# Attention and SwiGLU block on one core: twelve early head pairs laid four tokens to a partition and turned by TensorE, weight sums contiguous in DRAM, reciprocals between two transposes, and new durations in the planner

## The chip, the core and the metric

The kernel runs on one core of a Trainium2 chip. The metric is the device time of one launch in microseconds (us). The kernel before took a median of 1483.65 us in three runs (1482.71 to 1483.81). A separate, profiled execution took 1484.42 us; its span, from the first to the last instruction, was 1482.6 us, so 1.8 us lie around the span. Times called "at 85.2" are us from the start of that span.

## What is computed

Queries, keys and values have shape (8 batches, 12 heads, 448 tokens, 64). Each head is normalised and attended, the heads are joined to rows of 768, and the 3584 rows go through a SwiGLU block with 1536 hidden columns. All inputs but the weights are float32; the three weight matrices arrive as float64 words, which the kernel reads as pairs of 32-bit words and rounds itself.

```python
def rmsnorm(x, g):
    rms = np.sqrt(np.mean(x * x, axis=-1, keepdims=True) + 1e-06)
    return x / rms * g
q_n, k_n = (rmsnorm(q, g_q), rmsnorm(k, g_k))
scores = scale * np.matmul(q_n, k_n.transpose(0, 1, 3, 2))
attn = np.exp(scores - np.max(scores, axis=-1, keepdims=True))
attn = attn / (np.sum(attn, axis=-1, keepdims=True) + 1e-09)
x = np.matmul(attn, v)                      # then (B,H,S,D) -> (B*S, H*D)
g = x @ w_gate
return (g / (1.0 + np.exp(-g)) * (x @ w_val)) @ w_out
```

## The kernel before

**Stages.** Two heads of one batch are a *pair*; there are 48 pairs, m = 0 to 47. The first 12 pairs (EARLY, batches 0 and 1) are computed before any SwiGLU work. Then come four blocks, one for every two batches. A block has 120 up products (L1400: NG = 4 groups of hidden columns by 15 sums by gate and value, four matmul records each) and 30 down products (L1574: 15 sums by two halves of the output columns, eight records each). The products work on 15 sums and differences of input blocks with 15 sums and differences of weight blocks instead of the 18 plain ones, so the weights must be turned into "sides": `convert` loads 9 blocks of 128 columns, rounds them on ScalarE and VectorE, forms 11 sums on GpSimd and stores 15 blocks to DRAM (`up_sides`, `down_sides`). There are 24 conversions: 6 beside the early pairs, 18 beside the first block. `load_sides` (L1360) reads the sides back for each group of products, five sums at a time for up products and two for down products. The 36 late pairs run beside the down products of the blocks before the last.

**One pair** (`attention`). Queries and keys are loaded, squared (ScalarE, L767), summed (VectorE), turned into 1/rms (ScalarE L682 and L683, VectorE L688 to L690), scaled on GpSimd, and brought to the layout with the 64 head columns on the partitions, as KT and QT. Then four score tiles (j = 3, 0, 1, 2; L912), exponentials on ScalarE (L927), weighted values (L988) and column sums of the exponentials (L1019). For an early pair the sums are inverted on VectorE (L1054) and spread over the partitions by a TensorE product with a 0/1 matrix (L1062); for a late pair ScalarE spreads them by eight copies (L1072). ScalarE and VectorE add the two halves of the weighted values (L1077, L1080) and VectorE multiplies by the inverse (L1084).

There are two layouts on the way in. For a pair in NATURAL, which is pairs 0 and 1, a tile is [112 partitions, 2 heads, 4 tokens by 64]: one DMA with runs of 1 KB for queries and one for keys (L732). VectorE sums over 64 columns (L787). TensorE transposes four blocks of keys and four of queries into one PSUM tile of the ring `st` (L853); VectorE copies the keys out (L859), ScalarE the queries with the gain `gg` (L861). For all other pairs a tile is [4 strips of 32 columns, 14 by 32 tokens]: four DMAs with runs of 128 bytes each for queries and keys (L737); the sum over a head's 64 columns lies in two strips, so ScalarE swaps strips by four copies (L803) and VectorE adds (L807); the scaled tiles are turned by VectorE's 32 by 32 transposes (L865), and ScalarE scales the queries into QT (L868). The ring `st` has two tiles of two banks, and the score tiles take turns in it.

**At the start** TensorE is kept busy by four dummy products of 512 columns on the squared keys' input of pair 0 (L770). The keys of pair 0 are loaded from ScalarE's queue, everything else from SyncE's.

**Order.** No engine's order is written by hand. Every piece is given to a planner (`Order.add`: engine, duration, due time, what it comes after, which ring places it takes). `Order.run` plays the program with these durations and emits, again and again, the piece that can start first; among pieces that can start, the one with the earliest due time less `rank` (60 for early pairs, 20 for some conversions). Pieces of the same `group` on TensorE are kept together. Each engine executes in the emitted order, and a piece waits for what it needs. `SWITCH` is what a change of matmul mode costs in the play, `slack` a hop between engines; transfers were played as kilobytes over 300 GB/s plus 1.8 us.

Of the kernel before, what the change touches and what calls it, by code (L numbers as in the profile page):

```python
# [359 lines left out]

class Order:
# [10 lines left out]
    SWITCH = dict(PE=0.17, ACT=1.3)  # L372

    def __init__(self, pools, begin):
        self.begin = begin
        self.pools = {name: [None] * n for name, n in pools.items()}
        self.turn = dict.fromkeys(pools, 0)
        self.users = {}
        self.pieces = []
        self.free = {}  # L380
        self.port = 0.0
        self.dma = 0.0
        self.last = {}
        self.mode = {}

    def add(
        self, engine, us, when, emit, after=(), takes=(), uses=(), port=False, kb=0, group=None,
        mode=None, early=None, rank=0.0, slack=0.1,
    ):
        piece = dict(  # L390
            engine=engine, us=us, when=when, emit=emit, takes=takes, port=port, kb=kb,
            group=group, mode=mode, early=early, rank=rank, slack=slack,
# [10 lines left out]
    def start(self, piece):  # L403
# [6 lines left out]
        for before in piece["after"]:  # L410
            if before["end"] is None:
                return None
            at = max(at, before["end"] + piece["slack"] * (before["engine"] != piece["engine"]))
        for name, _ in piece["takes"]:
            old = self.pools[name][self.turn[name] % len(self.pools[name])]
            for user in self.users.get(old, ()):
                if user["end"] is None:
                    return None
                at = max(at, user["end"] + 0.1)
        return at  # L420

    def run(self, lookahead=400):
# [3 lines left out]
        while any(left.values()):  # L426
            best = None
            for engine, pieces in left.items():
# [15 lines left out]

                late = 0.7 if engine == "POOL" else 0.0
                if choice and (
                    best is None
                    or choice[0] + late < best[0] - 0.3
                    or choice[0] + late < best[0] + 0.3
                    and self.key(choice[1]) < self.key(best[1])  # L450
                ):
                    best = (choice[0] + late, choice[1])
# [8 lines left out]
            if piece["mode"] and self.mode.get(piece["engine"]) != piece["mode"]:  # L461
                end += self.SWITCH[piece["engine"]]
                self.mode[piece["engine"]] = piece["mode"]
                if piece["mode"] in self.begin:
                    self.begin[piece["mode"]]()
            self.last[piece["engine"]] = piece
# [3 lines left out]
            if piece["kb"]:  # L470
                self.dma = max(self.dma, end) + piece["kb"] / 300.0
                end = self.dma + 1.8
# [5 lines left out]
def fast(  # L478
# [60 lines left out]
    NATURAL = (0, 1)  # L539
# [9 lines left out]
        qk=4, v=2, t=2, QT=2, KT=2, e=4, ea=7, eh=2, sums=1, inv=1, rd=1, rows=3, st=2, at=2, ss=2,  # L549
# [65 lines left out]
    up_sides = [dram.tile([P, 15, 2, NC2, P], F32, name=f"up_sides{g}") for g in range(NG)]  # L615
    down_sides = dram.tile([P, 15, 2, NG, P], F32, name="down_sides")
# [58 lines left out]
    def inverse_root(m, sums, of, when, rank=0.0):  # L675
# [9 lines left out]
        def improve():  # L685
# [7 lines left out]
            "ACT", 0.5, when, estimate, after=[sums], uses=[("ss", m)], takes=[("rr", m)],  # L693
# [3 lines left out]
            "DVE", 0.45, when + 1.0, improve, after=[first], uses=[("ss", m), ("rr", m)],  # L697
# [9 lines left out]
    def attention(m):  # L707
# [19 lines left out]
        def load(x, src):  # L727
            def emit():
# [11 lines left out]
            both = m == 0 and src is k  # L740
            queue = nc.scalar if both else nc.sync
            return add(
                "ACT" if both else "SP", 0.5 if natural else 1.4 if both else 2.4, ready - 28.0, emit, takes=[("qk", (m, x))], kb=224, early=25.0,
# [15 lines left out]
        load_v = add("SP", 2.4, ready - 16.0, load_values, takes=[("v", m)], kb=256, early=25.0)  # L759

        def square(x):
# [6 lines left out]
            if m == 0 and x:  # L768
                for _ in range(4):
# [3 lines left out]
        for x in range(2):  # L773
            squares.append(
                add(
                    "ACT", 0.53, ready - 18.0, lambda x=x: square(x),
# [28 lines left out]
        def both():  # L805
# [6 lines left out]
            "DVE", 1.1, ready - 17.0, summed, after=squares, uses=[("t", m)], takes=[("ss", m)]  # L812
        )
        if not natural:
            sums = add("ACT", 0.9, ready - 16.0, swap, after=[sums], uses=[("ss", m)])
            sums = add("DVE", 0.15, ready - 15.0, both, after=[sums], uses=[("ss", m)])
# [6 lines left out]
        def scale(x):  # L823
            if natural:
# [16 lines left out]
                "POOL", 1.0, ready - 9.0, lambda x=x: scale(x), after=[rr], port=True,  # L841
# [32 lines left out]
        if natural:  # L874
            of_turned = ("st", (m, "turned"))
            kt, qt = [
                add(
                    "PE", 0.8, ready - 6.0, lambda x=x: turn(x), after=[scaled[1 - x]],
                    uses=[("t", m)] + [of_turned] * (1 - x), takes=[of_turned] * x, mode="full",
                )  # L880
                for x in (1, 0)
            ]
            kt = add(
                "DVE", 0.64, ready - 5.0, lambda: drain(1), after=[kt], takes=[("KT", m)],
# [3 lines left out]
                "ACT", 0.6, ready - 5.0, lambda: drain(0), after=[qt, gains], takes=[("QT", m)],  # L888
# [3 lines left out]
            "DVE", 0.62, ready - 6.0, lambda: transpose(1), after=scaled[:1], takes=[("KT", m)],  # L892
# [3 lines left out]
            "DVE", 0.62, ready - 6.0, lambda: transpose(0), after=scaled[1:],  # L896
# [3 lines left out]
            "ACT", 0.65, ready - 5.0, queries, after=[qt, gains], uses=[("qk", (m, 0))],  # L900
# [42 lines left out]
        for j in (3, 0, 1, 2):  # L943
# [4 lines left out]
                "PE", 0.41 if half else 0.76, when, lambda j=j: scores(j),  # L948
# [5 lines left out]
                "ACT", 0.5 if half else 0.92, when + 1.0, lambda j=j: exps(j),  # L954
# [3 lines left out]
            if j in (1, 2) and not early:  # L958

                def more_sums(j=j):  # L960
                    if j == 1:
# [5 lines left out]
                        "POOL", 2.15, when + 2.0, more_sums, after=[ex[j], ex[0], *adds[-1:]],  # L967
# [62 lines left out]
        for j in range(NJ):  # L1030
            half = j == NJ - 1
            last = add(
                "PE", 0.41 if half else 0.76, when + 0.01 * j, lambda j=j: weighted(j),
# [8 lines left out]
            "PE", 1.68 if early else 0.42, when + (0.05 if early else 0.3), total,  # L1042
# [10 lines left out]
        def invert():  # L1053
            nc.vector.reciprocal(take("rd", m, [P, Q]), tiles[den])  # L1054
# [27 lines left out]
        def divide():  # L1082
# [4 lines left out]
            "ACT", 0.55, when + 3.0, copy_sums, after=[last, up_done.get(b // 2 - 1)], uses=at[:1]  # L1087
# [683 lines left out]
```

## Time and profile before

| | before |
|---|---|
| median of three runs | 1483.65 us |
| profiled execution, its span | 1484.42 us, 1482.6 us |
| TensorE (PE) busy | 1435.1 us, 97% of the span |
| VectorE (DVE), ScalarE (ACT), GpSimd (POOL) busy | 914.8, 680.7, 416.0 us |
| mean TensorE clock granted | 0.992 |
| moved by DMA | 193.30 MB in 409457 packets, of them 316804 under 512 bytes |
| up products, two groups of 960 matmul records | 400.6 and 401.0 us busy |
| down products, three groups, 960 records | 177.2, 152.1 and 50.4 us busy |

The busy time of TensorE is the union of modelled intervals: a matmul record lasts longer than the distance to the next one, so a stretch can be called fully busy and yet not run at its best pace. For that the distance between starts is the better measure: in the trace four records of 64 by 64 matmuls of 448 columns start together every 0.375 us, and a 128 by 128 record of 448 columns starts every 0.376 us. "Idle before" in a group of instructions says how long the engine had nothing before them, and what ended that wait.

### The profile page before, as it was taken

Reading aid. Unit: us, or ns where it says so; the run is one execution under the profiler, and the core shown is the slowest. Engines: PE = TensorE matmul, PEld = TensorE weight load, DVE = VectorE, ACT = ScalarE, POOL = GpSimd, SP = SyncE. Lnnn points to the kernel's source line nnn. Section 1 sums busy time; section 2 is a strip of 40 time slices with the busy share of each in tenths; the row PEclk is TensorE's granted clock in tenths of the full one; section 3 lists DMA queues with packets and bytes.
Section 4 is the critical chain, followed back from the end, with each engine's and each line's share of the span. In section 5 each row is a group of like instructions: output and inputs, shape, how many; then the busy total and the mean of one; then the engine's idle time right before and its main releaser. Section 6 shows DMA issues by size and latency. Waiting matters only on the chain.

```text
span 1482.6 us, 19482 instructions
## 1 busy us (share of the span) xinstructions
PE 1435.1 (97%) x6696; PEld 680.7 (46%) x6696; DVE 914.8 (62%) x1403; ACT 680.7 (46%) x1358; POOL 416.0 (28%) x470
## 2 busy tenths in 40 slices
PE   6989999999999999999999999999999999999998
PEld 2434554443444455544444445554444445555553
DVE  3878897877978544355886733454786753432533
ACT  5864544437775321445767422354676532122100
POOL 3545585636444100012534200011343410000000
PEclk8999999999999999999999999999999999999999
DMA  6677999974453431533344432352444442222235
GB/s 166 160 162 215 294 331 335 289 213 92 98 117 84 111 107 71 144 98 89 78 110 107 101 118 72 110 132 77 97 101 103 89 123 85 80 98 73 83 98 107
DMA packets 409457, 193.30 MB, mean 130 GB/s; under 512 B 316804, under 2 KB 391428, under 8 KB 403204
## 3 DMA queue, kind: packets, MB, share of 16 engines
q1 hardware_dynamic: 397840, 190.35, 47.8%
q10 hardware_dynamic: 11380, 1.61, 0.7%
q8 instruction: 55, 0.90, 0.3%
q14 instruction: 54, 0.44, 0.1%
q0 software_dynamic: 128, 0.00, 0.0%
HBM read 157.29 MB, written 34.60 MB: 129 GB/s over the span
## 4 chain that ended last, share of the span: by engine, by line
PE 73%; ACT 3%; DVE 3%; issue 1%; DMA 1%; SPq 1%; ACTq 0%; DVEq 0%
PE mm L1574 22%; PE mm L1400 20%; PE at L1400 20%; PE st L912 6%; PE at L988 5%; PE st L1019 1%; ACT spare L1072 1%; ACT es L927 1%; SPq L737 1%; DVE rd L1054 1%; DVE ss L807 0%; DMA work<-in_k_dram 0%; DMA out_dram<-spare 0%; DVE ss L793 0%; ACT ss L803 0%
## 5 line engine op out<-in xcount | busy, mean ns | idle before, releaser
L1400 PE MATMUL at<-xs,ws 128*128 128x448 f32 x960 | 400.6, 540 | 4.3 <-DVE v L1346 3.1
L1400 PE MATMUL mm<-xs,ws 128*128 128x448 f32 x960 | 401.0, 540 | 3.6 <-DVE spare L1348 2.2
L1400 PEld LDWEIGHTS at<-xs,ws 128*128 128x128 f32 x960 | 181.9, 190 | 184.8 <-issue 172.1
L1400 PEld LDWEIGHTS mm<-xs,ws 128*128 128x128 f32 x960 | 181.6, 190 | 184.3 <-issue 172.0
L834 POOL TENSOR_TENSOR work<-work,rr 128x448 f32<-128x448 f32 x92 | 101.8, 1126 | 480.1 <-DVE rr L690 353.3
L1574 PE MATMUL mm<-gt,ws 128*128 128x448 f32 x448 | 177.2, 545 | 0.0
L912 PE MATMUL st<-work 64*64 64x448 f32 (+1 forms) x1536 | 156.4, 514 | 18.0 <-ACT es L927 7.5
L1344 DVE TENSOR_TENSOR gt<-gt,mm 128x448 f32<-128x448 f32 x64 | 39.7, 620 | 184.2 <-PE mm L1400 181.9
L1574 PE MATMUL mm<-hs,ws 128*128 128x448 f32 x384 | 152.1, 545 | 0.9 <-DVE ss L688 0.9
L927 ACT ACTIVATE es<-st 128x896 f32<-128x896 f32 x129 | 114.1, 912 | 54.3 <-PE at L988 42.6
L932 POOL TENSOR_TENSOR sums<-es 128x896 f32<-128x896 f32 x36 | 75.8, 2104 | 196.0 <-PE st L1019 83.4
L1474 ACT ACTIVATE st<-gt 128x448 f32<-128x448 f32 x96 | 52.3, 546 | 168.9 <-DVE gt L1348 90.3
L1072 ACT COPY spare<-rd 32x224 f32<-32x224 f32 x288 | 108.1, 375 | 35.4 <-DVE rd L1054 31.1
L1574 PEld LDWEIGHTS mm<-gt,ws 128*128 128x128 f32 x448 | 82.9, 190 | 84.2 <-issue 80.6
L988 PE MATMUL at<-es,v 64*64 64x448 f32 x1032 | 109.9, 544 | 2.7 <-DVE ss L688 2.5
L1342 ACT COPY gt<-mm 128x448 f32<-128x448 f32 x80 | 42.5, 532 | 140.4 <-PE mm L1400 140.4
L1574 PEld LDWEIGHTS mm<-hs,ws 128*128 128x128 f32 x384 | 71.1, 190 | 72.9 <-issue 70.6
L912 PEld LDWEIGHTS st<-work 64*64 64x64 f32 x1536 | 50.8, 135 | 98.8 <-issue 38.1
L1342 ACT COPY v<-at 128x448 f32<-128x448 f32 x96 | 51.1, 532 | 85.1 <-PE at L1400 81.0
L932 POOL TENSOR_TENSOR sums<-sums,es 128x896 f32<-128x896 f32 x36 | 78.7, 2186 | 2.8
L865 DVE STREAM_TRANSPOSE work<-work 128x448 f32<-128x448 f32 x92 | 56.6, 627 | 25.5 <-POOL work L834 22.8
L988 PEld LDWEIGHTS at<-es,v 64*64 64x64 f32 x1032 | 39.5, 134 | 63.0 <-issue 58.7
(161 smaller groups left out, 1589.1 us busy)
## 6 DMA issues: line engine op xcount, KB each, us to landing
ws<-up_sides SPq DMA_DIRECT2D x32, 1024.0 KB, 5.0
ws<-down_sides SPq DMA_DIRECT2D x16, 1024.0 KB, 5.0
ws<-down_sides SPq DMA_DIRECT2D x28, 512.0 KB, 4.3
ws<-up_sides SPq DMA_DIRECT2D x16, 768.0 KB, 4.4
work<-in_q_dram SPq DMA_DIRECT2D x184, 56.0 KB, 2.4
work<-in_k_dram SPq DMA_DIRECT2D x184, 56.0 KB, 2.4
out_dram<-spare SPq DMA_DIRECT2D x168, 56.0 KB, 1.9
v<-in_v_dram SPq DMA_DIRECT2D x96, 96.0 KB, 2.6
```

The costliest lines, as they stand in the source:

```text
L834: nc.gpsimd.tensor_tensor(out=tiles["t", m][:, x], in0=tiles["qk", (m, x)], in1=rr.to_broadcast([P, NC, C]), op=ALU.mult,)
L865: nc.vector.transpose(to, tiles["t", m][:, x].rearrange("p c f -> p (c f)"))
L912: nc.tensor.matmul(st[ds(D * x, D), h, 0:n], tiles["KT", m][rows, ds(P * j + D * of_keys, D)], tiles["QT", m][rows, ds(Q * of_queries, n)] ...
L927: nc.scalar.activation(e, tiles["st", (m, j)][:, :, 0 : S * width(j) // P], AF.Exp)
L932: nc.gpsimd.tensor_tensor(out=to, in0=tiles["e", (m, 0)] if j == 1 else to, in1=e, op=ALU.add)
L988: nc.tensor.matmul(tiles["at", (m, x)][ds(D * h, D), queries], tiles["v", m][rows, j, h], tiles["e", (m, j)][rows, h], start=j == 0, stop= ...
L1072: nc.scalar.copy(inv[ds(D * h + C * to, C), ts(x, Q)], tiles["rd", m][ds(D * h + C * x, C)])
L1342: nc.scalar.copy(to, ps)
L1344: nc.vector.tensor_tensor(out=to, in0=old, in1=ps, op=ALU.add)
L1400: nc.tensor.matmul(ps(), w[:, at, which, c], xs[:, SLOT[x], c], start=fresh and c == 0, stop=c == NC2 - 1, skip_group_check=True,)
L1474: nc.scalar.activation(take(*act, [P, 2, TB])[:, 0, 0:S], to, AF.Silu)
L1574: nc.tensor.matmul(banks[s][:, 0:S], w[:, at, s, g], where[x][:, g], start=fresh and g == 0, stop=g == NG - 1, skip_group_check=True,)
```

## The change

The diff does six things.

1. `NATURAL` holds all 12 early pairs instead of two. For the ten pairs 2 to 11, queries and keys come by one DMA each; the swap and its addition, the two VectorE transposes and the ScalarE scaling go; eight TensorE transposes, one VectorE copy and one ScalarE copy with the gain come.
2. The keys of pair 0 are loaded from SyncE's queue, and the dummies are three products on the queries of pair 0 instead of four on its keys.
3. The sides lie in DRAM with the 15 sums innermost but one ([P, 2, NC2, 15, P] instead of [P, 15, 2, NC2, P]). A conversion stores one run of 7680 bytes per partition, loaded sides come in four (up) or eight (down) runs of 512 bytes for each sum in a group. The tiles in SBUF and the matmuls' weight addresses follow.
4. For every pair, early or late, VectorE transposes the sums, inverts one column in 32 (7 per partition instead of 224), and transposes the broadcast back.
5. The planner's durations are new for almost every piece, a hop between engines costs 0.15, a mode switch 0.1, and a transfer is played by its issues, its packets and eight places in flight. GpSimd's handicap of 0.7 is gone, and the search for an engine's next piece ends at the first one that can start at once.
6. All conversions have rank 20; before, the first six had rank 0.

```diff
+def transfer(rows, size):
+    return rows * (6.64 + 0.045 * min(size, 4096)) / 16000.0
...
-    SWITCH = dict(PE=0.17, ACT=1.3)
+    SWITCH = dict(PE=0.1, ACT=1.3)
+    HOP, ISSUE, LANDING, PLACES = 0.15, 0.54, 2.0, 8
...
-            at = max(at, before["end"] + piece["slack"] * (before["engine"] != piece["engine"]))
+            at = max(at, before["end"] + self.HOP * (before["engine"] != piece["engine"]))
...
                     if choice is None or at < choice[0] - 0.4:
                         choice = (at, piece)
-
-                late = 0.7 if engine == "POOL" else 0.0
+                    if choice[0] <= self.free.get(engine, 0.0):
+                        break
...
+            for us in piece["moves"]:
+                place = self.issues % self.PLACES
+                at = max(at, self.landed[place]) + self.ISSUE
+                self.dma = max(self.dma, at - self.ISSUE + self.LANDING) + us
+                self.landed[place] = self.dma + 0.35
+                self.issues += 1
+                end = at
...
-    NATURAL = (0, 1)
+    NATURAL = (0, 1, 2, 3, 4, 5, 6, 7, 8, 9, 10, 11)
...
-    up_sides = [dram.tile([P, 15, 2, NC2, P], F32, name=f"up_sides{g}") for g in range(NG)]
-    down_sides = dram.tile([P, 15, 2, NG, P], F32, name="down_sides")
+    up_sides = [dram.tile([P, 2, NC2, 15, P], F32, name=f"up_sides{g}") for g in range(NG)]
+    down_sides = dram.tile([P, 2, NG, 15, P], F32, name="down_sides")
...
-            both = m == 0 and src is k
+            both = m == 0 and src is k and not natural
...
-            if m == 0 and x:
-                for _ in range(4):
+            if m == 0 and x == 0:
+                for _ in range(3):
                     nc.tensor.matmul(banks[0], chosen[0:R, 0], of, start=True, stop=True)
...
         def invert():
-            nc.vector.reciprocal(take("rd", m, [P, Q]), tiles[den])
+            rd, rc = take("rd", m, [P, Q]), take("rc", m, [P, Q // C])
+            nc.vector.transpose(rd, tiles[den])
+            nc.vector.reciprocal(rc, rd.rearrange("p (c i) -> p c i", i=C)[:, :, 0])
+            every = rc.rearrange("p (c one) -> p c one", one=1).to_broadcast([P, Q // C, C])
+            nc.vector.transpose(rd, every)
...
         inv = add(
-            "DVE", 1.52, when + 4.0, invert, after=[all_sums], uses=[] if of_bank else [den],
-            takes=[("rd", m)],
+            "DVE", 1.05, when + 4.0, invert, after=[all_sums], uses=[] if of_bank else [den],
+            takes=[("rd", m), ("rc", m)],
         )
         if early:
             inv = add(
-                "PE", 0.82, when + SPREAD, spread_by_product, after=[inv], mode="full", slack=1.0,
+                "PE", 0.75, when + SPREAD, spread_by_product, after=[inv], mode="full",
...
-        rank = 20.0 if by_bank else 0.0
+        rank = 20.0 if by_bank else 20.0
...
         last = add(
-            "SP", 0.6, when, lambda: nc.sync.dma_start(to, sides), after=[last], kb=960,
+            "SP", 0.6, when, lambda: nc.sync.dma_start(
+                to.rearrange("p x f -> p (x f)"), sides.rearrange("p x f -> p (x f)")
+            ), after=[last], moves=[transfer(2 * P, 3840)],
         )
...
-                src = sides[:, ds(first + here[0], size)]
-                nc.sync.dma_start(to[:, ds(i, size)], src.rearrange("p x a b f -> p x (a b f)"))
+                src = sides[:, :, :, ds(first + here[0], size)].rearrange("p a b x f -> p (a b) (x f)")
+                nc.sync.dma_start(to[:, :, ds(i, size)].rearrange("p n x f -> p n (x f)"), src)
```

## Prediction

> **What bounds the kernel now.** I read the page first, then busy time by stage, then what TensorE waited for in the first stage, then the timeline of the gaps.
>
> ```profile
> span 1482.6 us, 19482 instructions
> ...
> PE 1435.1 (97%) x6696; PEld 680.7 (46%) x6696; DVE 914.8 (62%) x1403; ACT 680.7 (46%) x1358; POOL 416.0 (28%) x470
> ```
>
> TensorE sets the end. A gain must come from its idle time, its slow clock or less work for it. This is the table by stage; columns are wall time, busy time of each engine, granted clock, DMA share, GB/s:
>
> ```profile
> 0.00:20.00 20.00, 11.06 (x39) 5.33 (x40) 6.59 (x20) 6.54 (x12) 7.46 (x18) 0.91 0.72 161
> 20.00:40.00 20.00, 14.42 (x144) 5.35 (x146) 9.50 (x19) 15.45 (x31) 3.68 (x4) 0.83 0.62 162
> ...
> 60.00:80.00 20.00, 17.42 (x201) 8.16 (x194) 16.50 (x28) 15.73 (x30) 13.21 (x22) 1.00 0.79 185
> 80.00:100.00 20.00, 16.84 (x174) 7.40 (x170) 12.33 (x20) 13.62 (x27) 9.39 (x16) 0.83 0.71 161
> ...
> 140.00:330.00 190.00, 184.28 (x490) 92.23 (x489) 156.59 (x234) 84.79 (x118) 118.93 (x228) 1.00 0.95 293
> 330.00:480.00 150.00, 145.16 (x967) 60.69 (x966) 122.03 (x178) 106.66 (x248) 77.11 (x46) 1.00 0.46 102
> 480.00:1440.00 960.00, 953.88 (x3931) 458.21 (x3930) 523.02 (x797) 397.62 (x821) 158.02 (x98) 1.00 0.37 99
> ```
>
> From 480 to 1440 only 6 us of 960 are idle. The gaps, and a clock of 0.83, lie in the first 140 us, where ten of the twelve early pairs are edited. What TensorE waited for there (total, times, longest):
>
> ```profile
> PE mm L770 <- DMA work<-in_k_dram: 6.8, 1, 6.8
> PE st L912 <- ACT es L927: 5.1, 2, 3.2
> PE st L912 <- ACT more L927: 4.1, 2, 3.2
> PE st L912 <- ACT work L861: 2.6, 2, 2.1
> PE at L988 <- DVE ss L688: 2.5, 1, 2.5
> ```
>
> The exponentials named are not the cause; they were only last. The timeline has it:
>
> ```profile
> 13.41 0.93 PE L853 MATMUL st<-ident,work 112*128 112x112 f32 x8
> ...
> 15.77 0.63 ACT L861 ACTIVATE work<-st,gg 128x448 f32<-128x448 f32 x1 [3.13 <-DVE gg L1680]
> 16.45 1.05 PEld L912 LDWEIGHTS st<-work 64*64 64x64 f32 x16 [2.32 <-ACT work L861]
> ```
>
> ```profile
> 87.86 0.58 ACT L767 ACTIVATE work<-work 128x448 f32<-128x448 f32 x1 [1.84 <-DMA work<-in_k_dram]
> 87.95 2.10 SPq L737 DMA_DIRECT2D work<-in_q_dram  x4
> 88.35 0.53 ACT L927 ACTIVATE more<-st 128x448 f32<-128x448 f32 x1
> ```
>
> At 87.86 ScalarE stands before a square whose keys have not landed; the exponentials behind it start late, and TensorE has been idle since 85.2. At 73.2 it is the same (square of late keys at 71.72, then 2.6 us idle). At the head, first scores are at 16.45 because the dummies hold TensorE to 13.41 and `gg` comes late on VectorE.
>
> Distances between matmul starts give the account from 16.45 to the first up product at 139.9, 123.5 us. Four 64 by 64 records of 448 columns start every 0.375 us, so a pair takes 2.63 (scores) + 2.63 (weighted) + 1.5 (sums) + 0.75 (spread) = 7.5 us: 90 for twelve, 0.8 for the transposes of pair 1. Gaps over 0.3 us and stretches at half clock are 22.6. The remaining 10 are mode switches and short waits, 0.8 a pair.
>
> **What the Trainium skill says.** TensorE: Matmul & The Clock Gate, "What's actually happening": after an idle window of about 3.4 us the clock falls to half. The trace agrees: after idling 3.4 us at 24.8 and 3.3 us at 85.2 the distance is 0.75 instead of 0.375 us, which cost some 2.7 and 3.0 us. "Part 4: PE-mode transpose" of that page adds that transposes do not count as activity; no trace of before can show that, as only 16 were made. DMA: Bandwidth & Descriptors, "Specifications", names 512 bytes as the least size for line rate. Here a 128-byte packet took 12.5 ns in the first 140 us and a 1024-byte one 52, so 1 KB goes in 52 instead of 100 ns. SBUF — State Buffer, "SBUF: two separate sides": a VectorE operation with two SBUF inputs and a GpSimd one exclude each other; the tiny L807 agrees, 400 ns mean where undisturbed ones took 190.
>
> **The change, part by part**, in us of the end; each estimate with both ends.
>
> *Head.* Keys of pair 0 were issued on ScalarE's queue at 1.61 behind the gains and landed after 5.1 us; now they are SyncE's second transfer, ahead of the values. Queries landed after about 3. Keys may land at 4.5 to 6.7; I take 5.5. From landing to scaled queries took 5.4 us for the first pair's last scale (6.71 to 12.1). The six dummy records at half clock, 0.857 each, end at about 9 instead of 13.4, before that. Then transposes 0.4, copy 0.63, hops: scores at 12.9, a gain of 3.5. With `gg` late again it is 0, with keys at 4.5 it is 5.5. **−3.5 (−5.5 to 0).**
>
> *Transposes on TensorE, ten pairs.* Eight in 0.76 (one every 0.095 at 13.41). Keys and queries come from two scales 1.0 apart on GpSimd, so there are up to two visits; a visit into full mode and out cost 0.35 around L1062. Without any visit of their own they cost 7.6, with two 14.6, at half clock 18. Search now ends at the first piece that can start, so a due transpose breaks a group of scores: I take 1.26 each. All of this is on the path where TensorE is busy. **+12.6 (7.6 to 18).**
>
> *Waits that go.* Per pair ScalarE loses 0.88 (swap) and 0.67 (L868), gains 0.63 (L861) and 0.1 on squares: −0.8. VectorE loses 1.24 (two L865), 0.19 (L807), gains 0.62 (L859), 0.15 (L787 over L793), 0.17 (L791): −0.5; the reciprocal, 1.55, becomes two transposes of half of 0.62 with overhead and a tiny one, 0.85 to 1.05, so −0.6 more. GpSimd pays 0.2 more (1.02 against 0.92 a scale). SyncE issued eight DMAs a pair in about 4 us, now two in about 1.1, and the loads of values and weights in that queue move up. DMA time falls from 27.9 us for 35840 short packets to 4480 times 52 over 16 engines, 14.6. So late keys at 71.7 and 87.9, and the ramp between 20 and 28 (pair 2 squared at 22.7, its keys' issue done only at 16.1) should go, with the slow clock after. Next late is ScalarE: 6.1 a pair plus 2.6 a conversion, about 8 in 9.5. In front of it now stands the query copy, which waits for TensorE; behind it queue exponentials. The turned tile also takes one of two score tiles for about 2.3 us (second scale 1.0, transposes 0.4, copy 0.63, hops); I cover that by 4.9 us of weighted values, sums and spread of the pair before. Of 22.6 I expect 14 to go; if only the head's ramp is mended 4, if almost all 19. **−14 (−19 to −4).**
>
> *Sides, conversions, first block.* A store is 1920 packets of 512 bytes at 28.7 ns, 3.4 us over 16 engines; in 3840-byte ones at the rate of 4096 (191 ns) 3.1. Loads of 8192 bytes at 387 ns become runs of 512 to 2048 at 29 to 86: within 0.7 us a load either way. No TensorE wait from 140 to 330 ends on these; loads are due 24 us ahead: nothing. If that cover failed, 0.7 for 92 loads would be 64 us of DMA, not of TensorE. Rank 20 lets the first six conversions pass pairs 9 to 11: sides for the first block are stored before 115, when before the fourth was. Gaps over 0.3 in the first block's up products sum to 6.5 us, each ended by a VectorE read queued behind conversions (the longest 2.25 at 236), and 330 to 480 has 4.8 idle us where 480 to 1440 has 6 in nearly three blocks. Truer durations should take some. **−4 (−8 to +4).**
>
> *Late pairs.* The shorter reciprocal hides beside down products (TensorE waited 1.3 us for L1054 in all). Reordering can break groups: two more visits at 0.2 for a third of 36 pairs is 5. **−1 (−4 to +5).**
>
> The sum is −3.5 + 12.6 − 14 − 4 − 1 = −9.9. Against the profiled 1484.4 that is 1474.5; the median lies 0.8 under that execution: 1474.
>
> **Rivals.** (a) *Slower: the ring of score tiles.* The cover of 4.9 us fails where scores are next in order, and TensorE waits for the turned tile. The other terms leave 9.9, so a cost of 1.0 for each of ten pairs decides. If most of the 2.3 us counts, 1.8, the end is +8: 1492. For it: the stage has stretches without a gap (54.4 to 63.4 is one pair in 9.05). Against: TensorE's other work. (b) *Given back.* The stage ends earlier but the first block waits for conversions: VectorE is busy 157 of 190 us there, GpSimd 119, DMA 0.95. The gain of 5 in the first stage and the 4 return as waits: 1484. Against it: three of the four sets of sides aren't needed at once. (c) *More.* Transposes slip into waits (7.6), 19 of stalls go, the first block and the late pairs give 8 and 2: −3.5 + 7.6 − 19 − 10 = −25, so 1459. For it: of the span, 2880 product records at 0.376 (1083), 36 late pairs at 5.6 (203) and twelve early at 7.5 (90) leave 107 us that are neither. That the layouts don't do what they say is excluded for loads (pairs 0 and 1 have it already).
>
> **Chances.** Forecast 0.51 (own range 1465 to 1480), (c) 0.20, (b) 0.10, (a) 0.19. Less than 0.2%, 3 us, can't be told from no change here. Faster 0.71, same 0.10, slower 0.19. The range 1459 to 1489 leaves out half of (c) below and half of (a) above.
>
> **What would show it.** First scores near 13; first up product near 135; no L737 load before 140; granted clock 1.0 between 80 and 100; L853 with 96 records; L1054 near 0.2 us; stores without 512-byte packets. Wrong it would be if first up products come after 140, if L912 waits for L861 or L859 in every pair, or if gaps from 480 on grow past 10 us.

## Result and profile after

The changed kernel took a median of 1478.07 us in six runs (1474.53 to 1478.83), the one before 1483.73 us in six (1482.71 to 1485.8). The ratio is 0.9958 with a 95% interval of 0.9948 to 0.9968: 5.7 us less, where 9.9 were forecast. The profiled executions lie further apart, 1476.75 against 1484.42, because that of after lies 1.3 under its median and that of before 0.7 over its own; the steps below are taken from these two and sum to 7.7.

The page of after, its span and the busy time of each engine:

```profile
span 1474.9 us, 19565 instructions
...
PE 1438.7 (98%) x6774; PEld 687.7 (47%) x6774; DVE 889.6 (60%) x1489; ACT 676.2 (46%) x1320; POOL 401.9 (27%) x470
```

TensorE is busy 3.6 us longer (the transposes are among it) in a span 7.7 us shorter. By stage (wall time, busy time of each engine, granted clock, DMA share, GB/s):

```profile
0.00:20.00 20.00, 11.78 (x42) 5.41 (x46) 7.71 (x21) 6.65 (x12) 7.48 (x18) 0.83 0.82 223
20.00:40.00 20.00, 15.33 (x152) 6.65 (x148) 12.04 (x24) 16.00 (x26) 4.09 (x4) 0.91 0.56 158
...
60.00:80.00 20.00, 19.99 (x249) 9.92 (x242) 14.80 (x32) 17.33 (x28) 10.14 (x16) 1.00 0.63 187
80.00:100.00 20.00, 19.94 (x260) 10.41 (x256) 16.07 (x31) 14.55 (x24) 10.44 (x16) 1.00 0.45 133
...
140.00:330.00 190.00, 186.87 (x503) 93.32 (x504) 156.18 (x239) 94.52 (x135) 113.29 (x218) 0.99 0.87 288
330.00:480.00 150.00, 146.83 (x984) 61.97 (x986) 119.51 (x192) 103.86 (x238) 68.32 (x44) 1.00 0.46 99
```

The slices from 60 to 100 have no idle TensorE and no slow clock any more. What is left sits at both ends of the first stage. The waits of TensorE from 0 to 140 (total, times, longest):

```profile
PE st L928 <- ACT es L943: 4.2, 2, 3.3
PE mm L787 <- DVE gp L1764: 4.0, 1, 4.0
PE st L870 <- POOL work L844: 2.4, 1, 2.4
PE st L1082 <- DVE rd L1074: 1.7, 1, 1.7
PE mm L1428 <- DVE xs L1145: 1.7, 1, 1.7
PE st L928 <- ACT work L878: 1.2, 3, 0.7
```

Of the signs that the forecast named, the transposes are 96 records, the reciprocal takes 0.20 us and the clock is 1.00 from 80 to 100. First scores came at 15.26 instead of near 13, the first up product at 137.28 instead of near 135. None of the signs of being wrong came: scores wait for the query copy (L878 here) three times and not in every pair, and the gaps from 480 to 1440 stayed at about 7 us.

Distances between matmul starts give the same account for every kernel; it is used in all that follows. "Gaps" are those over 0.3 us beyond what a matmul takes at full clock, so half clock counts in them, for matmuls of 448 columns and more. Times in us:

| | first scores at | to first up product (gaps) | up products, block 0 (gaps) | down products and pairs, block 0 (gaps) | the same, block 1 | span |
|---|---|---|---|---|---|---|
| before | 16.45 | 123.5 (22.3) | 188.4 (6.5) | 175.6 (7.1) | 164.9 | 1482.6 |
| after | 15.26 | 122.0 (11.6) | 189.5 (6.8) | 172.1 (5.0) | 163.0 | 1474.9 |
| turned_twice | 14.99 | 130.5 (13.1) | 191.0 (8.6) | 172.3 (5.1) | 163.0 | 1484.9 |
| undo_natural | 15.19 | 132.3 (29.0) | 192.0 (9.4) | 172.1 (5.0) | 163.3 | 1486.7 |
| plan_alone | 16.94 | 133.0 (30.0) | 208.8 (23.6) | 170.1 (6.3) | 163.8 | 1505.1 |
| edits_old_plan2 | 13.85 | 120.6 (12.9) | 196.4 (13.0) | 172.9 (6.2) | 162.2 | 1479.9 |
| undo_reciprocal | 15.11 | 124.8 (14.6) | 188.9 (6.1) | 178.2 (10.6) | 163.2 | 1483.5 |
| undo_sides | 15.11 | 122.1 (11.7) | 189.7 (6.9) | 172.2 (5.0) | 163.0 | 1475.0 |
| undo_rank | 15.36 | 131.7 (23.7) | 189.8 (7.4) | 172.1 (5.0) | 162.9 | 1483.8 |
| search_on | 15.26 | 127.5 (18.4) | 191.8 (8.9) | 171.8 (5.0) | 163.1 | 1481.8 |
| head_in_order | 12.62 | 122.8 (12.9) | 187.8 (5.3) | 172.1 (5.0) | 162.9 | 1471.3 |
| holds_in_order | 12.45 | 122.2 (12.1) | 186.1 (3.1) | 172.1 (5.0) | 162.9 | 1469.0 |

Blocks 1 and 2 are alike; the last block's 180.5 and the tail's 97.7 are the same in before and after.

The borders of this table are starts of products, and work can cross them. In before the last early pair's spread (0.75 us) lies behind the first up product, in after ahead of it. In after 1.1 us of a late pair's scores lie ahead of block 0's first down product, in before behind it.

### The profile page after: what moved, and what is told of

Its sections match the earlier page's. It is cut to its first block, busy times and chain, and to the rows that moved or that the text cites. A ratio compares the mean times of both kernels' runs of the same rounds, so it can differ in the third digit from the quotient of the medians.

```text
span 1474.9 us, 19565 instructions
## 1 busy us (share of the span) xinstructions
PE 1438.7 (98%) x6774; PEld 687.7 (47%) x6774; DVE 889.6 (60%) x1489; ACT 676.2 (46%) x1320; POOL 401.9 (27%) x470
## 4 chain that ended last, share of the span: by engine, by line
PE 76%; DVE 3%; ACT 2%; DMA 2%; issue 1%; SPq 0%; DVEq 0%; ACTq 0%
PE mm L1606 23%; PE at L1428 20%; PE mm L1428 20%; PE st L928 6%; PE at L1004 5%; PE st L1035 1%; DMA out_dram<-spare 1%; ACT es L943 1%; DMA ws<-up_sides 0%; ACT spare L1092 0%; DVE spare L1654 0%; DVE rr L706 0%; DVE st L1266 0%; DMA ws<-down_sides 0%; DVE sums L954 0%
## 5 line engine op out<-in xcount | busy, mean ns | idle before, releaser
L851 POOL TENSOR_TENSOR work<-work,rr 128x448 f32<-128x448 f32 x72 | 73.4, 1041 | 467.2 <-DVE rr L706 370.0
L928 PE MATMUL st<-work 64*64 64x448 f32 (+1 forms) x1536 | 154.3, 511 | 10.5 <-ACT es L943 6.4
L1366 DVE TENSOR_TENSOR gt<-gt,mm 128x448 f32<-128x448 f32 x64 | 39.7, 621 | 189.7 <-PE mm L1428 186.5
L948 POOL TENSOR_TENSOR sums<-es 128x896 f32<-128x896 f32 x36 | 75.3, 2093 | 188.9 <-ACT es L943 61.3
L948 POOL TENSOR_TENSOR sums<-sums,es 128x896 f32<-128x896 f32 x36 | 75.6, 2099 | 2.8
L1366 DVE TENSOR_TENSOR v<-v,at 128x448 f32<-128x448 f32 x64 | 39.7, 620 | 40.9 <-PE at L1428 40.9
```

What stands on the lines that cost most here:

```text
L851: nc.gpsimd.tensor_tensor(out=tiles["t", m][:, x], in0=tiles["qk", (m, x)], in1=rr.to_broadcast([P, NC, C]), op=ALU.mult,)
L928: nc.tensor.matmul(st[ds(D * x, D), h, 0:n], tiles["KT", m][rows, ds(P * j + D * of_keys, D)], tiles["QT", m][rows, ds(Q * of_queries, n)] ...
L948: nc.gpsimd.tensor_tensor(out=to, in0=tiles["e", (m, 0)] if j == 1 else to, in1=e, op=ALU.add)
L1366: nc.vector.tensor_tensor(out=to, in0=old, in1=ps, op=ALU.add)
```

## The experiments

Two theories stood against each other. Mine: each part does what its own term says, so undoing it gives the term back. The rival: the parts change an order, and a part is worth what the plan makes of it together with the others. Line numbers in the sections below are those of each kernel's own profile, a few lines off those of after. Each ratio is to executions of before from the same session; the distances to after are between medians (before's own median moved from 1483.57 to 1484.12 between the sessions).

### The layout alone, undone

```diff
-    NATURAL = (0, 1, 2, 3, 4, 5, 6, 7, 8, 9, 10, 11)
+    NATURAL = (0, 1)
```

> The changed kernel, but only pairs 0 and 1 laid four tokens to a partition; planner, sides, reciprocals and dummies stay new. My account (transposes cost about 9 us of TensorE, the waits that go give 11): first up product about 1.5 us later than the changed kernel's 137.3, the end 0 to 3 us later, so about 1479. Rival, the planner alone mended the gaps: the 9 us of transposes and switches come off, first up product near 129, end near 1470. Second rival, the layout is worth much more than the account shows: first up product past 145, end past 1484.

Measured: 1488.56 us, ratio to before 1.0025 (1.0014 to 1.0035); 10.5 us over after, as the second rival said, with the first up product at 147.44. TensorE's largest waits in the first 140 us:

```profile
PE st L928 <- ACT work L885: 7.1, 4, 2.8
PE at L1004 <- DVE xs L1100: 4.2, 1, 4.2
```

L885 is ScalarE's scaling of queries behind VectorE's transposes, which the new layout does not have; gaps in the stage are 29.0 instead of 11.6 us. So under the new plan the layout pays for its transposes and 10 us more. It is even slower than before, where the same layout ran under the old plan.

### The plan alone

Nearly everything that is executed is as before (layout, dummies, sides, reciprocal, keys of pair 0 from ScalarE's queue); the planner, its durations and rank 20 are the new ones, and only what a planned piece costs follows the old instruction: 1.55 for the reciprocal, 512-byte runs for the store.

> The kernel before in what is executed for each pair and conversion, planned by the new planner with the new figures. My account: about 1479 to 1481, with the late blocks as short as in the changed kernel (163.0 us for the second block's down products with their pairs, 164.9 before) and the first stage as before (first up product at 140). Rival, planner mends the first stage: first up product near 130, end near 1473. Rival, planner gives nothing without the edits: 1484.

Measured: 1505.55 us, 1.0143 (1.013 to 1.0157), 22 us slower than before, and slower than any of the three forecasts. The first stage has gaps of 30.0 us, and the first block's up products 23.6 instead of 6.5. TensorE's largest waits from 140 to 500:

```profile
PE st L928 <- ACT work L885: 5.9, 1, 5.9
PE mm L1421 <- DVE gt L1365: 4.7, 1, 4.7
PE mm L1421 <- DVE gt L1361: 4.0, 1, 4.0
```

"Truer durations should take some" of the waits is refuted where nothing else is changed. Undone first, the layout is the smaller part of the loss: undo_natural has the old layout too and is 17 us faster. In the table nearly all of that, 16.8 us, lies in block 0's up products (192.0 and 208.8; 1.5 of it is more late scores that crossed the border). Between the two stand the reciprocal, the sides, and the queue and dummies of pair 0.

### The edits under the old plan

The converse: the planner, figures and ranks of before (1.05 for the reciprocal apart), with all executed edits. One rule of order is taken over from after: a pair's queries are turned after its keys. Without that rule the old planner turned the queries of pair 7 before the tile that keys and queries share was there.

> The kernel before with every edit to what is executed, planned by the planner and figures of before (1.05 for the reciprocal; the queries' transposes come after the keys' in the plan). Two runs have shown that layout and planner can't be added up: the new planner without the layout had its first up product at 147.4, with the layout at 137.3. Theory A, the layout itself is worth some 10 us whatever the planner: first up product near 130, end near 1474. Theory B, the layout only repairs what the new planner loses, and the old planner had nothing to repair: first up product at 138 to 142, end at 1480 to 1486. Theory C, the old figures play the new layout wrongly: first up product past 145, end past 1488.

Measured: 1480.55 us, 0.9975 (0.9967 to 0.9984): 3.1 us less than before. The first up product starts at 134.49, 2.8 us earlier than in after, but the first block's up products take 196.4 us with gaps of 13.0, against 188.4 and 6.5 before. (Another 1.1 are a late pair's scores, as in after.) That is rival (b) of the forecast, given back. In this one trace 3.0 us more than in the others lie behind the last block (100.7 instead of 97.7 to 97.9), after all arithmetic had ended; the trace doesn't show why. So the edits alone bring 3, the plan alone costs 22, and together they bring 5.7: the terms are not additive, and the rival theory is the better one for these two parts. Theory B had the end right, but not the stage: its first up product was to come at 138 to 142.

### Transposes doubled

Each of pairs 2 to 11 is turned twice, 80 matmul records more; the second turn repeats the first, and the order is that of after.

```diff
-            for j in range(NJ):
+            for j in [*range(NJ)] * (2 if m > 1 else 1):
```

> The changed kernel with each of the eight transposes of pairs 2 to 11 made twice, in the same order of all engines. If TensorE sets the pace of the first stage, eighty more transposes at 0.095 us are 7.6 us: first up product at 144 to 145, end 7 to 8 us later. If the transposes lie in waits, at most 2 us later. If the ring of score tiles is the limit, more than 10 us later, since the turned tile is held 0.76 us longer in each pair and TensorE waits beside it.

Measured: 1484.1 us, 0.9999 (0.999 to 1.0007), 6.0 us over after by the medians. In the profiled executions the first up product moves from 137.28 to 145.45, 8.2 us; that of turned_twice is the slowest of its runs, so 6.0 to 8.2 is what can be said. 80 records at 0.095 are 7.6. So transposes lie on the path, as forecast, and the second turn costs about its own matmuls. It pays for no visit of its own, so it doesn't show what the first visit costs. Each pair holds its tile 0.8 us longer, and at most 0.6 us in all is left beyond the matmuls up to the first up product: holding a tile of the ring longer (rival (a)) costs next to nothing here.

### Sides as before

DRAM and SBUF layout of the sides, the store and the loads as before; the planned cost is kept, so that the order is that of after.

> The changed kernel with the sides in DRAM laid out as before (fifteen stores of 512 bytes per partition in a conversion, longer runs on loading), in the same order of all engines. My forecast costed the layout at nothing: within 1 us of the changed kernel. Rival, DMA is short in the first block (share 0.87 to 0.95): 24 stores at 0.4 to 0.8 us and later loads make it 3 to 10 us slower, all of it from 140 to 330.

Measured: 1476.96 us, 0.9955 (0.9939 to 0.9972), with executions from 1475.03 to 1479.21 where after's lie from 1474.53 to 1478.83. DMA share from 140 to 330 is 0.93 with the old runs and 0.87 with the new ones, and TensorE waits for such a load once, 0.5 us with the old runs: worth nothing, as forecast.

### Reciprocal as before

```diff
-            rd, rc = take("rd", m, [P, Q]), take("rc", m, [P, Q // C])
-            nc.vector.transpose(rd, tiles[den])
-            nc.vector.reciprocal(rc, rd.rearrange("p (c i) -> p c i", i=C)[:, :, 0])
-            every = rc.rearrange("p (c one) -> p c one", one=1).to_broadcast([P, Q // C, C])
-            nc.vector.transpose(rd, every)
+            nc.vector.reciprocal(take("rd", m, [P, Q]), tiles[den])
+            take("rc", m, [P, Q // C])
```

It is planned at the new 1.05, so the order is that of after, while the instruction takes 1.55.

> The changed kernel with one reciprocal of 224 columns per pair (1.55 us) in place of transpose, reciprocal of 7 columns, transpose, in the same order of all engines. Forecast: late pairs hide it, in the first stage VectorE has 0.5 more per pair, 12 pairs, of which a third shows: 1 to 3 us slower, before the first up product. Rival, VectorE bounds the first stage: 6 us slower. Rival, it hides everywhere: 0.

Measured: 1485.25 us, 1.0013 (1.0007 to 1.0019), 7.2 us over after, where I expected 1 to 3, and all before the first up product. In the traces, 8.6 us apart, 2.7 lie there, as I expected, and 6.1 in the down products of block 0 with their pairs. TensorE's waits from 140 to 500 hold these two:

```profile
PE st L928 <- DVE rd L1070: 4.7, 3, 2.0
PE mm L1603 <- DVE spare L1367: 1.7, 1, 1.7
```

Scores wait for an inverse, which they don't read: a late pair's sums lie in a tile of the ring `st`, and the tile comes free only when VectorE has taken them. In after the first of them is 1.7 us (two times) and the second isn't there, so waits make 4.7 of the 6.1. The other 1.4 are four matmul distances at half clock behind the wait of 2.0 us. I had written that this reciprocal "hides beside down products" from the 1.3 us of waits named after it in before. In before the order was planned for 1.52; here it is planned for 1.05, and the true 1.55 stands open. The run shows the price of a wrong duration as much as that of the instruction, and doesn't part the two.

### Rank 0 for the first six conversions

```diff
-        rank = 20.0 if by_bank else 20.0
+        rank = 20.0 if by_bank else 0.0
```

> The changed kernel with rank 0 instead of 20 for the six conversions beside the early pairs, planned anew. If the rank is what lets conversions push VectorE's last early work back (it waits behind a conversion at 128 to 133), the first up product comes 1 to 4 us earlier and the first block pays it back or not: end 1474 to 1478. Rival, the sides for the first block come too late without it: first up product past 140, end past 1481.

Measured: 1485.17 us, 1.0006 (0.9999 to 1.0014), 7.1 us over after. Two waits, the first from 0 to 140 and the second after it:

```profile
PE st L1082 <- DVE rd L1074: 6.3, 1, 6.3
```

```profile
PE mm L1428 <- DMA ws<-up_sides: 7.3, 1, 7.3
```

With rank 20 the first is 1.7 us and the second isn't there. On VectorE additions for the first block's inputs (129.39 to 132.41) and six steps of a conversion (132.32 to 136.32) stand before the last pair's inverse at 136.76, and then the first block's weights come late. To see whether rank 20 needs the layout I crossed the two, and put rank 20 under the old plan as well:

> The changed kernel with only pairs 0 and 1 laid four tokens to a partition and with rank 0 for the first six conversions. Theory: rank 20 is only affordable because the layout takes 0.5 us of VectorE and 0.8 of ScalarE out of a pair; without the layout rank 20 is what put the first up product at 147.4, so with rank 0 it comes back to 139 to 142, end 1480 to 1484. Rival: the sides for the first block are the limit either way (the changed kernel with rank 0 waited 7.3 us for them), first up product at 148 or later, end 1489 or more.

> All edits to what is executed, planner and figures of before, but rank 20 for all conversions as in the changed kernel. With the old rank the first up product was at 134.5 and the first block's up products lost 13 us in gaps. Theory: those gaps are conversions that come too late, so rank 20 takes 5 us or more out of them and adds 0 to 3 to the first stage: end 1474 to 1479. Rival: rank 20 pushes the pairs' VectorE work back, first up product past 138, end 1481 or more.

Old layout and rank 0 under the new plan: 1490.77 us, 1.0046 (1.0034 to 1.0058), with the first up product at 157.46 instead of at 139 to 142. So without the layout rank 20 is worth 2.2 us (1490.77 − 1488.56), with it 7.1; my theory that it can be afforded only with the layout falls, since it doesn't cost without it. Under the old plan with all edits, rank 20 gives 1482.58 us, 0.999 (0.9982 to 0.9998), 2.0 us more than rank 0 by the medians, 1.5 by the ratios. I had expected 5 us or more off the first block's up products; they take 205.0 us instead of 196.4. The first up product comes at 131.65, the earliest of all runs, and the first block gives it back:

```profile
PE mm L1408 <- DMA ws<-up_sides: 9.2, 1, 9.2
PE mm L1408 <- DVE gt L1354: 3.1, 1, 3.1
```

### The search goes on past the first ready piece

```diff
-                    if choice[0] <= self.free.get(engine, 0.0):
-                        break
```

> The changed kernel planned without the early end of the search, so that a due transpose can't break a group of scores or weighted values that could go on. If broken groups are what the transposes cost beyond their 7.6 us, the first stage is 2 to 4 us shorter: end 1474 to 1476. If transposes that wait for the end of a group make exponentials late, it is longer: end 1480 or more. If the early end hardly ever decides: 1478.

Measured: 1483.91 us, 1.0000 (0.9992 to 1.0008), 5.8 us over after, with gaps of 18.4 instead of 11.6 in the first stage. I had feared that the early end would break groups of scores, at a cost. The run has it the other way round. By the code, the search without it goes on to a piece of the group that runs and passes over a ready one that is due; that this is where the 5.8 us come from was not followed piece by piece.

### Pieces that stand in the way, emitted later

In after's first 16 us I found three pieces on in-order queues in front of something that TensorE awaits. The plan stays; only the emission of these three is put off: pair 1's squares until pair 0's 1/rms is through ScalarE, pair 1's sums until pair 0's steps on VectorE are through, and pair 0's key copy until the queries' transposes.

```diff
+    def after_first(holds, what, emit):
+        if holds and held[what] is not None:
+            held[what].append(emit)
+        else:
+            emit()
...
-                    lambda x=x: square(x),
+                    lambda x=x: after_first(m == 1, "rr", lambda: square(x)),
...
-                "DVE", 0.62, ready - 5.0, lambda: drain(1), after=[kt], takes=[("KT", m)],
+                "DVE", 0.62, ready - 5.0, lambda: after_first(m == 0, "turned", lambda: drain(1)), after=[kt], takes=[("KT", m)],
```

> The changed kernel, planned as it is, but at emission pair 1's squares come behind pair 0's 1/rms on ScalarE, pair 1's sums behind pair 0's on VectorE, and the key copy of pair 0 behind the queries' transposes. In the changed kernel pair 0's Ln waited from 6.8 to 8.5 behind pair 1's squares, and its queries' transposes from 12.8 to 13.5 for the key copy. Expected: first scores at 12.5 to 13 instead of 15.26. If TensorE's work sets the pace of the first stage from there, first up product and end come 2 to 2.5 us earlier (1476). Rival, the ramp up to 27 us waits for pair 2's squares and the exponentials, not for pair 0: end unchanged.

Measured: 1474.39 us, 0.9941 (0.9928 to 0.9954), 3.7 us under after and faster than both kernels, with first scores at 12.62. Of the 3.6 us between the two traces, order accounts for 1.9: the first up product starts at 135.42 instead of 137.28, a little less than the 2 to 2.5 expected (2.6 at the first scores, of which the stage behind them lost 0.8 again). The other 1.7 is luck of the clock in block 0's up products. TensorE runs the same matmuls in the same order in both, and waits for the same read equally long. First after, then head_in_order:

```profile
278.40 2.40 PE L1428 MATMUL mm<-xs,ws 128*128 128x448 f32 x4 [2.88 <-DVE gt L1370]
```

```profile
276.52 1.77 PE L1448 MATMUL mm<-xs,ws 128*128 128x448 f32 x4 [2.88 <-DVE gt L1390]
278.12 1.67 PE L1448 MATMUL at<-xs,ws 128*128 128x448 f32 x4
```

In after half clock follows (starts 0.75 us apart from 279.8 to 282.8), in head_in_order it doesn't. Since the order had helped, four more pieces were put off in the same way: the divide of pair 10 behind the inverse of pair 11, side 6 behind side 8 (the first product takes side 8), and the second half of one down conversion, its sums on GpSimd too, behind the read that TensorE waited 2.9 us for.

```diff
-                    lambda k=k, op=op: op(k),
+                    lambda k=k, op=op: after_first(key == ("down", 5) and k == 1, "read9", lambda: op(k)),
```

> The changed kernel with the plan as it is and seven pieces emitted later than planned: the three of head_in_order, and four more that stood on VectorE in front of something that TensorE was waiting for. The divide of pair 10 now stands behind the reciprocal of pair 11, side 6 of the second half behind side 8 (the first product takes side 8), and the second half of one down conversion (three VectorE operations and the sums behind it on GpSimd) behind the read of the last up sum of the third group, for which TensorE waited 2.9 us at 273.6 in head_in_order. Theory (what is left of the early stage and of the first block is order, not work): waits of 2.9, 0.6 of 1.7 and 1.0 of 1.7 us go and 1.5 us of half clock with the first, 5 to 6 us together: median 1468 to 1470, up products of the first block 184 to 185 us instead of 187.8. Rival (given back): the conversion that is held is needed later on, its sums come 2.3 us later and the down products wait for it, or the read behind is late next: the median stays at 1473 to 1475 and the gap moves.

Measured: 1470.81 us (1470.57 to 1472.04), 0.9915 (0.9902 to 0.9929): 3.6 us less again by the medians (2.3 between the traces), 13 us under before. I expected 5 to 6. The wait of 2.9 us became two, in TensorE's timeline:

```profile
272.39 1.77 PE L1458 MATMUL mm<-xs,ws 128*128 128x448 f32 x4 [0.49 <-DVE gt L1400]
275.18 1.77 PE L1458 MATMUL at<-xs,ws 128*128 128x448 f32 x4 [1.01 <-DVE v L1400]
```

So 1.7 us of that block went, and 0.8 in front of it (the first up product at 134.63 instead of 135.42). The other read behind the first is late next, as the rival said. And the 1.5 us of half clock that I counted on were not to be had: in the trace of head_in_order that wait had cost none.

## Why the prediction held, and where it didn't

**The head, −3.5 forecast, −1.2 measured: this term failed.** Keys landed by 4.7, sooner than the 5.5 that I took, and the dummies were out of the way by 9.5, before the first transpose at 11.83. But I followed pair 0 alone, and on each queue pair 1 stood in between. The timeline of after (start, duration, what; in brackets the idle time before it and what ended it):

```profile
8.00 0.63 ACT L784 ACTIVATE work<-work 112x512 f32<-112x512 f32 x1 [0.28 <-DMA work<-in_k_dram]
8.54 0.20 ACT L698 ACTIVATE rr<-ss 112x16 f32<-112x16 f32 x1
...
10.83 0.97 DVE L705 SCALAR_TENSOR_TENSOR ss<-ss,rr 112x16 f32<-112x16 f32 x1
...
11.84 0.97 DVE L706 SCALAR_TENSOR_TENSOR rr<-ss,rr 112x16 f32<-112x16 f32 x1
12.73 0.14 DVE L1712 SCALAR_TENSOR_TENSOR gg<-gq,gk 128x1 f32<-128x1 f32 x1
12.80 0.61 DVE L876 COPY work<-st 128x448 f32<-128x448 f32 x1
...
13.55 0.98 PE L870 MATMUL st<-ident,work 112*128 112x112 f32 x4 [1.12 <-DVE work L876]
```

At 8.00 the square of pair 1 waits for a load to land, with pair 0's logarithm (8.54) behind it. At 10.83 and 11.84 two small steps of pair 1 stand in front of pair 0's key copy, and they take 0.97 us each because GpSimd is scaling pair 0 at the same time. At 13.55 the queries' transposes wait for that copy, since keys and queries share one tile of `st`. With these three out of the way head_in_order has its first scores at 12.62, where the forecast had 12.9: the edits could do what I said, the order did not let them.

**Transposes +12.6 and stalls −14: net right, both too large.** The stage from first scores to first up product went from 123.5 to 122.0, −1.5 where the two terms gave −1.4. Gaps fell from 22.3 to 11.6, so 10.7 of the 14 went; the transposes and all else in the stage then cost 9.2. Of this, 0.75 is the last pair's spread, which crossed the border; 8.4 remain, where 80 transposes alone are 7.6 and doubling gave 6.0 to 8.2. I had added 0.5 us of visits for each pair; less than 0.1 of it is left, as far as the stage's other work stayed what it was. The −1.5 is luck in part: two misses of 3 to 4 us offset each other. The stalls named in the forecast (squares behind late keys) are gone: after 20 us ScalarE waits 0.5 us in all for keys or queries before a square, and the clock from 80 to 100 is 1.00. The ramp is the one that stayed, in another form:

```profile
22.65 2.18 ACT L784 ACTIVATE work<-work 112x512 f32<-112x512 f32 x4
...
25.35 0.21 ACT L698 ACTIVATE rr<-ss 112x16 f32<-112x16 f32 x1 [0.53 <-DVE ss L808]
...
25.72 0.90 ACT L943 ACTIVATE es<-st 128x896 f32<-128x896 f32 x1
...
26.67 0.94 PE L928 MATMUL st<-work 64*64 64x448 f32 x4 [3.26 <-ACT es L943]
```

Four squares and a logarithm of coming pairs stand before the exponentials of the pair at hand, and TensorE is idle 3.26 us. The loads are in time now; the order on ScalarE is not. TensorE: Matmul & The Clock Gate, "What's actually happening", puts the fall of the clock after about 3.4 us of idling. Here 3.26 us of waiting was followed by six distances of score records in 4.00 us instead of the 2.25 of full clock, so slightly less was enough. In these traces the length of a wait alone doesn't decide: half clock followed a wait of 2.0 us in undo_reciprocal and one of 2.88 in after, but not the same wait of 2.88 in head_in_order.

**First block with its down products −4, measured −2.4; late pairs −1, measured −2.7.** Up products of block 0 lost 1.1 and its down products gained 3.5, but 1.1 of both is the late pair's scores that crossed the border, and the spread that crossed into the stage before takes 0.75 from the up products. Without these the up products lost 0.7 (0.3 of it in gaps, 6.8 instead of 6.5), the down products gained 2.4 (gaps of 5.0 instead of 7.1), and the −2.4 is −1.7. Blocks 1 and 2 gained 1.9 and 2.0 in their down products and lost 0.6 twice in up products. Here I credited "truer durations" and priced the reciprocal at nothing. The runs say otherwise: the new plan alone costs 15 us net in these two stretches of block 0 (plan_alone, 20.4 more and 5.5 less), and the reciprocal is worth 6.1 in the second of them as planned.

The measured terms sum to −1.2 − 1.5 − 2.4 − 2.7 = −7.8, the 7.7 of the two spans within rounding. Rival (a), the ring, did not come up. Rival (b), given back, did, in the runs with all edits under the old plan. Rival (c), more, was out of after's reach, but holds_in_order is 7 us faster than after by order and, in the traces, 1.7 us of clock.

The total was right, in its direction and within about 4 us, but not for the reason that I gave: I added six edits as if each were worth its own work. The range held partly because errors offset each other. The parts interlock: under the new plan the layout is worth 10.5, rank 20 7.1, the reciprocal 7.2, the end of the search 5.8, the sides about 0; these sum to 30.6 where the whole brought 5.7. The other side of that sum is in part the new plan, which holds two of these parts itself and is 22 us slower alone. **Open** remains which of its new figures loses so much without the executed edits (they were not put back one by one). Open too is how much of the reciprocal's 7.2 is left when it is planned at its true 1.55, and what the queue and the dummies of pair 0 are worth, as they were never undone alone.

## What to carry to other kernels

When the order on the engines comes from a planner, price an edit by the order it leads to: keep the plan and change the instruction, then keep the instructions and change the plan, before adding the terms. Look on every in-order queue at what stands directly in front of the piece that the bound engine waits for, the next tile's preparation above all; putting off seven such pieces brought 7.3 us by the medians, more than the six edits (in the traces 5.9, of which 1.7 is clock). Before crediting an edit, see whether the clock fell after the same wait in both traces. A buffer's holder can wait for an operation whose result nobody reads at that moment (scores for an inverse), so an operation is hidden only as long as its tile isn't wanted.

## What the runs showed of the hardware

- L705 took 0.97 us at 10.83, and 0.17 at 10.21. SBUF — State Buffer, "SBUF: two separate sides", has it that a VectorE operation with two SBUF inputs and a GpSimd one exclude each other; a GpSimd scale of 1.02 us began at 10.73, which agrees. A tiny operation pays a whole neighbour, and at the head that is on the path.
- The reciprocal took 1.55 us for 224 columns and 0.20 for 7. Two transposes of 128 by 224 at 0.41 and the small inverse make 1.02, a third less.
- Eighty transposes more left the granted clock about where it was: 0.991 to 0.996 in turned_twice's thirteen executions, 0.990 to 0.997 in after's six. Whether transposes count as activity can't be read from stretches of 0.76 us between other matmuls.
- One and the same kernel moves by 4.3 us (after, 1474.53 to 1478.83), and its fastest execution has the highest granted clock, 0.997. One wait of 2.88 us was followed by about 3 us of half clock in after and by none in head_in_order.
- Stores of 7680-byte runs and loads of 512 to 2048, instead of stores of 512 and loads of 2048 to 8192, changed the DMA share from 140 to 330 by 0.06 and the time by nothing that shows.
